# Reordering the beginning of a fused Fourier-filter and MoE kernel: x on one queue, zeros on TensorE, filters in x's place, weights' bits off GpSimd's queue

## The chip, the cores and the metric

The kernel runs on one core of one Trainium2 chip. A core has five engines that take their own instruction streams in order: TensorE (PE in the profile; PEld is its weight load), VectorE (DVE), ScalarE (ACT), GpSimd (POOL) and SyncE (SP). SP, ScalarE and GpSimd can each issue DMAs from their stream; "SPq" is SP's part as a queue of DMA issues. The metric is the device time of one execution in microseconds; the time before is 2791.76 us, the median of three runs (2789.57 to 2792.46).

## What is computed

The reference, cut to what matters (x and the filters are float32, the two weights arrive as 64-bit floats and the kernel computes in float32; eight batches of 3008 positions and 256 channels; hidden width 2048):

```python
X = np.fft.rfft(x, axis=1)                 # x: (8, 3008, 256)
F = (filt_r + 1j * filt_i)[None, :, :]     # (1505, 256)
y = np.fft.irfft(X * F, n=3008, axis=1)
t = y.reshape(24064, 256)
h = t @ w_in                               # (256, 2048)
g = h * np.clip(h + 3.0, 0.0, 6.0) / 6.0
out = g @ w_out                            # (2048, 256)
```

## The kernel before

**The Fourier part.** 3008 = 47 x 64, so each transform is done in two factors as matrix products with constant tables. For a batch, `a_unit` multiplies the 47 rows of x (for two halves of 32 columns j) with table `wa`; the result goes to DRAM as `z_tmp` (`z_store`) and comes back with another axis on the partitions (`t2_load`). `b_unit` (L350) multiplies with table `wb`, `f_unit` (L362 to L364, VectorE) applies the filter tile `ft`, `bi_unit` (L382) goes back with table `wi`, `g_store` writes `g_tmp` in DRAM. `t4_load` (L413) reads it back, and `n_unit` (L420) makes the last product with `wai` and leaves transposed tokens in `xn`, which the MoE part reads in blocks of 512. `wb` and `ft` come in six parts c of four frequencies (`table_load`: four filter DMAs and one of `wb`); two buffers of each exist (`FB` = 2).

**The first batch** takes another way into this, since nothing can hide it. `x0_load` reads batch 0 into 94 partitions (rows 0 to 46 for the half h = 0, 47 to 93 for h = 1), 28 of its 32 columns in the upper part of `w_all` (the place of the MoE weights, not yet filled) and 4 in a `t1` tile. h = 0 goes through SP's queue and h = 1 through ScalarE's. `a0_unit` (L295) multiplies each column with the 96-wide table in `start`, four columns to a PSUM bank, four banks in turn; ScalarE copies them (L297) into `xn` and `xs`, used as scratch. `turn` (L307) transposes them with an identity to where `b_unit` wants them, in place of the trip through DRAM. Then six rounds c follow, each with `turn(c+1)`, two `b_unit` and `f_unit`, and `bi_unit` and `g_store` of the round before, the stores from ScalarE's queue.

**The weights.** The 16 parts of `w_in` and `w_out` (eight pairs p) are loaded as pairs of 32-bit integer words ("bits", 512 KB each) and decoded to float32 by seven or eight VectorE operations (`w_conv`, L222 to L240), called a conversion here. Two are converted before the rounds, two within them, two after them and ten in the first steps of the MoE part. Their loads go through GpSimd's queue by default. `w_sums` (L247, GpSimd) then makes eight sums for a pair, which overwrite slot 1 of `w_in` and of `w_out`; so they are made two steps after the pair's plain use.

**The MoE part** is a loop over 47 blocks k and eight pairs p. Block 0 is plain: `plain_up` (L532), the activation (L490 on ScalarE, `hswish` L495 on VectorE), `plain_down` (L543). All later blocks use a seven-product scheme (L445 up, L521 down) which needs the sums. Other work is hung on numbered steps (k*8 + p) by `at(step, fn, ...)`; work of the same step runs in the order in which it was entered, `a_unit`, `b_unit`, `bi_unit` and `n_unit` early in the step and all other late. Batch 1's `a_unit` and `z_store` stand in steps 1 to 8, its first `b_unit` in step 11. The block's result goes out by `store`, 14 DMAs for block 0 on SP.

The order within each engine is the order of the program text (`manual_schedule`), and a queue's DMA that waits holds all that is behind it.

Of the kernel before, what the change touches and what calls it, by code (L numbers as in the profile page):

```python
# [32 lines left out]
HC = NC // 2  # L33
XC = 4
# [20 lines left out]
def _make_tables():  # L55
# [5 lines left out]
    for h in range(2):  # L61
        for k in range(KH):
            th = 2 * np.pi * ((a * k) % NA) / NA
            for g in range(2):
                wa[h * 64:h * 64 + NA, g * 64 + k] = np.cos(th)
                wa[h * 64:h * 64 + NA, g * 64 + 32 + k] = -np.sin(th)
            start[h * NA:(h + 1) * NA, P + 4 * k + h] = np.cos(th)
            start[h * NA:(h + 1) * NA, P + 4 * k + 2 + h] = -np.sin(th)
# [39 lines left out]
def kernel(  # L108
# [60 lines left out]
    def table_load(b, c):  # L169
        t = ft[(b * NT + c) % FB]  # L170
# [4 lines left out]
        wb = tabp.tile([P, TC, P], FP32, name="wb")  # L175
# [68 lines left out]
    def w_sums(p):  # L244
        for w, sums in ((w_in[p], IN_SUMS), (w_out[p], OUT_SUMS)):
            for o, x0, x1, op_ in sums:
                nc.gpsimd.tensor_tensor(out=w[:, o, :], in0=w[:, x0, :], in1=w[:, x1, :], op=op_)  # L247
# [11 lines left out]
    IN_SUMS = ((4, 1, 3, ALU.add), (1, 0, 1, ALU.subtract), (5, 4, 0, ALU.subtract), (6, 2, 5, ALU.subtract))  # L259
    B11, T3, B21, B22, T1, T2, T4 = range(7)  # L260
    OUT_SUMS = tuple((o, x0, x1, ALU.subtract) for o, x0, x1 in ((4, 1, 0), (1, 1, 3), (5, 3, 4), (6, 2, 5)))
# [13 lines left out]
    def x0_tile(j):  # L275
        if j < 28:
            return w_all.rearrange("p a b c m -> p (a b c m)")[:, 4 * 14 * P:].rearrange("p (j d) -> p j d", d=D), j
        return st["x0"], j - 28

    def x0_load(j, n):  # L280
        t, o = x0_tile(j)
        rows = x[0].rearrange("(a c) d -> a c d", c=NC)
        for r, m in ((0, 32), (32, NA - 32)):
            for h, q in ((0, nc.sync), (1, nc.scalar)):
                q.dma_start(t[h * NA + r:h * NA + r + m, o:o + n, :], rows[r:r + m, ds(h * HC + j, n), :])
# [4 lines left out]
    def a0_unit(j):  # L290
        for dh in range(2):
            ps = bank(0)
            for u in range(4):
                t, o = x0_tile(j + u)
                nc.tensor.matmul(ps[:, ds(u * 96, 96)], t[0:2 * NA, o, ts(dh, P)], st["start"][0:2 * NA, ds(P, 96)],  # L295
                                 start=True, stop=True)
            nc.scalar.activation(out=zt(dh).rearrange("p (n j) -> p j n", j=HC)[:, j:j + 4, :],  # L297
                                 in_=ps[:, 0:384].rearrange("p (j n) -> p j n", j=4), func=AXT.Copy)
# [34 lines left out]
    def z_store(b, c):  # L333
        t = st.pop(("t1", b, c))
        for g in range(2):
            for ri in range(2):
                p0 = g * 64 + ri * 32
                z = z_d[b, :, ts(ri, NC), :].rearrange("k (h j) d -> k h j d", h=2)
                nc.gpsimd.dma_start(z[:, :, ds(c * XC + 2 * g, 2), :], t[p0:p0 + KH, :, :, :])  # L339
# [14 lines left out]
    def f_unit(b, i):  # L354
        c, r = divmod(2 * i, TC)
        ps = st.pop(("ps", b, i))
        f = ft[(b * NT + c) % FB][:, r:r + 2, :]
# [50 lines left out]
    def t4_load(i, k0=0, k1=KH):  # L408
        b, j, n = chunks[i]
        for h in range(2):  # L410
            for ri in range(2):
                p0 = h * 64 + ri * 32
                nc.sync.dma_start(t4[i % 2][p0 + k0:p0 + k1, 0:n, :].rearrange("k j d -> k (j d)"),  # L413
# [197 lines left out]
    with tc.manual_schedule():  # L611

        st["start"] = p14p.tile([P, 2, 2, P], FP32, name="p14").rearrange("p a u m -> p (a u m)")
        st["x0"] = t1p.tile([P, 2, XC // 2, D], FP32, name="t1").rearrange("p a j d -> p (a j) d")
        nc.sync.dma_start(st["start"][:, 0:2 * P], start_d)
        nc.vector.memset(top_c, -0x40000000)
        nc.vector.memset(half_c, 0.5)
        for j in range(0, 24, 8):  # L620
            x0_load(j, 8)
        for j in 24, 28:
            x0_load(j, 4)
# [3 lines left out]
        def convert(n, act=True, most=NCONV, q=nc.gpsimd):  # L627
            nonlocal loaded, done
            for i in range(n + 1):
# [3 lines left out]
                if i < n:  # L633
                    w_conv(done, act)
                    done += 1

        convert(0, most=2)
        for t in t4:
            nc.gpsimd.memset(t, 0.0)
        for c in range(FB):  # L640
            table_load(0, c)
            convert(0, most=3 + c, q=nc.sync)
        for j in range(0, HC, 4):
            a0_unit(j)
        convert(2, False, 4)
        turn(0)
        for c in range(NT + 1):
            if c + 1 < NT:
                turn(c + 1)
            if c < NT:  # L650
# [3 lines left out]
                if c + FB < NT:  # L654
                    table_load(0, c + FB)
                if c in (1, 3):
# [178 lines left out]
```

## Time and profile before

| what | us |
|---|---|
| median of three runs | 2791.76 |
| the profiled execution | 2791.65 |
| its span, first to last instruction | 2789.9 |
| TensorE busy | 2714.4 (97%) |
| VectorE busy | 1940.1 (70%) |
| ScalarE busy | 1330.6 (48%) |
| GpSimd busy | 398.4 (14%) |

The marks of the beginning, by start in the timeline:

| mark | us |
|---|---|
| first L295 pass | 8.0 |
| first ScalarE copy L297 | 22.9 |
| first L307 pass | 44.4 |
| first L350 pass | 51.5 |
| last issue of a g_tmp store by ScalarE | 90.9 |
| first psn pass (L420) | 104.4 |
| first plain pass (L532) | 110.2 |
| first pass of the seven-product scheme (L445) | 187.3 |
| first L350 pass of batch 1 | 218.6 |

A float32 matmul shows as two passes in the trace, so counts there are twice those of the program. A row such as "PE po L295 <- ACT xn L297: 8.7, 1, 8.7" reads: TensorE stood for 8.7 us in total before instructions of line 295, once, until a ScalarE instruction of line 297 released it. The rows that carry the argument are shown with the prediction.

### The profile page before, as it was taken

How to read it: one execution, taken by the hardware profiler on the slowest of the kernel's cores; microseconds unless marked ns; L12 is line 12 of the kernel's file. 1: busy time of each engine (PE TensorE's matmuls, PEld its weight loads, DVE VectorE, ACT ScalarE, POOL GpSimd, SP SyncE). 2: the span in 40 equal slices, each digit the busy share in tenths (PEclk: the TensorE clock that was granted, in tenths of full speed). 3: DMA queues.
4: the chain of work that ended last, by engine and by line, in shares of the span. 5: the costliest groups of instructions: out<-in, count | busy, mean ns of one | idle time of the engine just before them, and what ended most of it. 6: DMA issues, size and time to landing. Idle time of an engine off the chain costs nothing.

```text
span 2789.9 us, 47067 instructions
## 1 busy us (share of the span) xinstructions
PE 2714.4 (97%) x18112; PEld 2420.2 (87%) x18112; DVE 1940.1 (70%) x3399; ACT 1330.6 (48%) x2663; POOL 398.4 (14%) x627
## 2 busy tenths in 40 slices
PE   7698999999999999999999999999999999999997
PEld 6367888989889998899988998899988999999997
DVE  3656765777657776677756777567775677766665
ACT  3233445454554445544455445544455444444443
POOL 0170112010120011201021101210012100000000
PEclk9899999999999999999999999999999999999999
DMA  6633223321323222322133221332123321110000
GB/s 156 190 85 108 66 62 85 85 77 44 80 60 90 74 53 71 88 62 79 46 88 87 72 57 46 86 91 71 49 55 91 98 60 47 36 31 23 19 9 16
DMA packets 117321, 194.73 MB, mean 70 GB/s; under 512 B 21843, under 2 KB 83251, under 8 KB 116687
## 3 DMA queue, kind: packets, MB, share of 16 engines
q1 hardware_dynamic: 93561, 136.24, 17.2%
q0 software_dynamic: 19456, 50.52, 7.8%
q10 hardware_dynamic: 4080, 4.96, 0.7%
q8 instruction: 143, 2.34, 0.4%
q14 instruction: 81, 0.66, 0.1%
HBM read 119.80 MB, written 71.83 MB: 69 GB/s over the span
## 4 chain that ended last, share of the span: by engine, by line
PE 93%; DVE 3%; DMA 2%; SPq 1%; POOL 1%; issue 0%; ACT 0%; POOLq 0%; ACTq 0%; DVEq 0%
PE po L521 41%; PE al L445 22%; PE be L445 17%; PE psn L420 4%; PE psf L350 3%; PE psf L327 2%; PE psf L382 2%; PE po L295 1%; DMA w_all<-in_x_dram 0%; SPq L413 0%; DVE g L495 0%; PE po L350 0%; DMA out_dram<-o 0%; DMA wb<-wb_t 0%; DVE y L224 0%
## 5 line engine op out<-in xcount | busy, mean ns | idle before, releaser
L521 PEld LDWEIGHTS po<-w_all,g 128*128 128x128 f32 x10304 | 1368.7, 191 | 143.4 <-issue 36.5
L521 PE MATMUL po<-w_all,g 128*128 128x128 f32 x10304 | 1399.1, 276 | 3.7 <-DVE g L495 3.3
L495 DVE SCALAR_TENSOR_TENSOR g<-r,h 128x512 f32<-128x512 f32 x736 | 506.7, 688 | 268.2 <-ACT r L490 255.2
L490 ACT ACTIVATE r<-h,half_c 128x512 f32<-128x512 f32 x736 | 531.1, 722 | 326.2 <-DVE h L471 314.1
L445 PE MATMUL al<-xt,w_all 128*128 128x256 f32 x2208 | 660.2, 381 | 1.5 <-DVE h L476 1.0
L471 DVE TENSOR_TENSOR h<-be,s 128x512 f32<-128x512 f32 x368 | 254.2, 691 | 271.4 <-PE be L445 260.0
L445 PE MATMUL be<-xn,w_all 128*128 128x256 f32 x1472 | 437.8, 379 | 0.0
L445 PEld LDWEIGHTS al<-xt,w_all 128*128 128x128 f32 x2208 | 335.5, 192 | 3.5 <-issue 1.3
L445 PEld LDWEIGHTS be<-xn,w_all 128*128 128x128 f32 x1472 | 279.7, 190 | 37.9
L485 ACT ACTIVATE h<-al 128x256 f32<-128x256 f32 x368 | 141.3, 384 | 350.5 <-PE al L445 350.5
L476 DVE TENSOR_TENSOR h<-al,s 128x256 f32<-128x256 f32 x368 | 156.3, 425 | 166.0 <-PE al L445 164.8
L503 DVE TENSOR_TENSOR g<-g 128x512 f32<-128x512 f32 x368 | 254.8, 692 | 12.6
L466 ACT ACTIVATE s<-al 128x256 f32<-128x256 f32 x368 | 141.4, 384 | 208.5 <-PE al L445 208.5
L457 ACT ACTIVATE s<-be 128x256 f32<-128x256 f32 x368 | 141.3, 384 | 176.4 <-PE be L445 176.4
L445 PE MATMUL al<-xn,w_all 128*128 128x256 f32 x736 | 219.9, 381 | 0.5 <-ACT h L485 0.5
L445 PE MATMUL be<-xt,w_all 128*128 128x256 f32 x736 | 218.9, 379 | 0.0
L339 POOL DMA_DIRECT2D z_tmp<-t x224 | 129.6, 583 | 412.1 <-ACT t L330 409.2
L456 ACT ACTIVATE s<-al 128x256 f32<-128x256 f32 x368 | 141.3, 384 | 71.0 <-PE al L445 71.0
L505 DVE TENSOR_TENSOR g<-g 128x256 f32<-128x256 f32 x368 | 160.8, 437 | 12.5
L502 DVE TENSOR_TENSOR g<-g 128x256 f32<-128x256 f32 x368 | 156.5, 425 | 12.6
L445 PEld LDWEIGHTS be<-xt,w_all 128*128 128x128 f32 x736 | 139.8, 190 | 18.9
L420 PEld LDWEIGHTS psn<-wai,t 128*128 128x128 f32 x1024 | 134.1, 195 | 22.2 <-issue 16.0
(106 smaller groups left out, 1793.5 us busy)
## 6 DMA issues: line engine op xcount, KB each, us to landing
t<-g_tmp SPq DMA_DIRECT2D x188, 120.0 KB
z_tmp<-t POOLq DMA_DIRECT2D x224, 96.0 KB, 2.9
t<-z_tmp SPq DMA_DIRECT2D x42, 512.0 KB
g_tmp<-t POOLq DMA_DIRECT2D x84, 256.0 KB, 3.8
out_dram<-o SPq DMA_DIRECT2D x321, 47.0 KB
xs<-in_x_dram SPq DMA_DIRECT2D x112, 128.0 KB
ft<-in_filt_r_dram SPq DMA_DIRECT2D x96, 128.0 KB
ft<-in_filt_i_dram SPq DMA_DIRECT2D x96, 128.0 KB
```

The costliest lines, as they stand in the source:

```text
L420: nc.tensor.matmul(ps[:, ts(q, TOK)], t4[i % 2][:, q, ts(dh, P)], wai[:, chunks[i][1] + q, :], start=True, stop=True)
L445: nc.tensor.matmul(ps, w_in[p][:, w, :], x, start=start, stop=stop, skip_group_check=True)
L456: nc.scalar.activation(out=s[:, 0, :], in_=al, func=AXT.Copy)
L466: nc.scalar.activation(out=s[:, 1, :], in_=al, func=AXT.Copy)
L471: nc.vector.tensor_tensor(out=st["h"][0].rearrange("p (a n) -> p a n", a=2), in0=be, in1=s, op=ALU.add)
L476: nc.vector.tensor_tensor(out=st["h"][1][:, 256:512], in0=al, in1=s5, op=ALU.add)
L490: nc.scalar.activation(out=r, in_=st["h"][i], func=AXT.Relu, bias=half_c, scale=1.0 / 6.0)
L495: nc.vector.scalar_tensor_tensor(out=st["g", k, p][:, o:o + 2, :].rearrange("p a n -> p (a n)"), in0=st["r", i], scalar=1.0, in1=st["h"][i ...
L502: v.tensor_tensor(out=g[:, G1, :], in0=g[:, G3, :], in1=g[:, G22, :], op=ALU.add)
L503: v.tensor_tensor(out=g[:, G3:G2 + 1:2, :], in0=g[:, G3:G1 + 1, :], in1=g[:, G11:G11 + 1, :].broadcast_to([P, 2, 256]), op=ALU.subtract)
L505: v.tensor_tensor(out=g[:, G4, :], in0=g[:, G12, :], in1=g[:, G2, :], op=ALU.subtract)
L521: nc.tensor.matmul(st["po", k][bank][:, part, u, :], g[:, a, ts(u, P)], w_out[p][:, w, :], start=(p == 0 and n in OPENS and u == 0), stop= ...
```

## The change

It has six parts. The first batch's x is loaded by SP alone, into partitions 0 to 46 and 63 to 109, in pieces of 4, 4, 8, 8 and 8 columns; partitions 47 to 62 get 16 rows of x once more, against which the table has zeros, so that a0 runs over 110 rows, and its products are 128 columns wide instead of 96. Five matmuls over a tile of zeros (one column of it is not zero) stand on TensorE ahead of a0, and ScalarE has a small copy ahead of its first real one. The filters and `wb` of rounds 2 to 5 are loaded into the place of x in `w_all`, all ahead of the rounds. Weights' bits are loaded through SP, but for the first two; three conversions stand before the rounds and two after, none within, and eleven in the MoE part; three sums follow each conversion and the fourth comes two steps after the use, as before. The first loads of `g_tmp` take 16 of 24 rows and stand a round earlier, and the rest goes through SP and ScalarE. Batch 1's `z_store` goes through SP, and its first two table loads stand in step 5 instead of step 9.

```diff
@@ -31,6 +31,7 @@
 DFF = 2048
 HALF = 64
 HC = NC // 2
+H1 = 63
 XC = 4
 NB = HC // XC
 TC = 4
@@ -64,8 +65,8 @@
             for g in range(2):
                 wa[h * 64:h * 64 + NA, g * 64 + k] = np.cos(th)
                 wa[h * 64:h * 64 + NA, g * 64 + 32 + k] = -np.sin(th)
-            start[h * NA:(h + 1) * NA, P + 4 * k + h] = np.cos(th)
-            start[h * NA:(h + 1) * NA, P + 4 * k + 2 + h] = -np.sin(th)
+            start[h * H1:h * H1 + NA, P + 4 * k + h] = np.cos(th)
+            start[h * H1:h * H1 + NA, P + 4 * k + 2 + h] = -np.sin(th)
     wb = np.zeros((P, KH, P))
     wi = np.zeros((P, 3, NC))
     re, im = slice(0, NC), slice(NC, P)
@@ -167,12 +168,17 @@
     def table_load(b, c):
-        t = ft[(b * NT + c) % FB]
+        if b == 0 and c >= FB:
+            at = x0_at(1536 * (c - FB), 1536)
+            t, wb = at[:, 0:1024].rearrange("p (k d) -> p k d", k=TC), at[:, 1024:].rearrange("p (k m) -> p k m", k=TC)
+        else:
+            t, wb = ft[(b * NT + c) % FB], tabp.tile([P, TC, P], FP32, name="wb")
+        st["ft", b, c] = t
         for src, p0 in ((filt_r, 0), (filt_i, HALF)):
             nc.sync.dma_start(t[p0:p0 + 32, :, :].rearrange("p k d -> p (k d)"),
                               raw(src, c * TC, [[NA * D, 32], [1, TC * D]]))
             nc.sync.dma_start(t[p0 + 32:p0 + 64, :, :], raw(src, NA - c * TC, [[NA * D, 32], [-D, TC], [1, D]]))
-        wb = tabp.tile([P, TC, P], FP32, name="wb")
         nc.sync.dma_start(wb, wb_d[:, ts(c, TC), :])
         st["wb", b, c] = wb
@@ -241,10 +247,10 @@
                                op0=ALU.is_ge, op1=ALU.mult)
-    def w_sums(p):
-        for w, sums in ((w_in[p], IN_SUMS), (w_out[p], OUT_SUMS)):
-            for o, x0, x1, op_ in sums:
-                nc.gpsimd.tensor_tensor(out=w[:, o, :], in0=w[:, x0, :], in1=w[:, x1, :], op=op_)
+    def w_sums(i, late):
+        w = (w_in, w_out)[i % 2][i // 2]
+        for o, x0, x1, op_ in (IN_SUMS, OUT_SUMS)[i % 2][3 * late:3 + late]:
+            nc.gpsimd.tensor_tensor(out=w[:, o, :], in0=w[:, x0, :], in1=w[:, x1, :], op=op_)
@@ -256,9 +262,9 @@
     A11, S3, A12, A22, S1, S2, S4 = range(7)
-    IN_SUMS = ((4, 1, 3, ALU.add), (1, 0, 1, ALU.subtract), (5, 4, 0, ALU.subtract), (6, 2, 5, ALU.subtract))
+    IN_SUMS = ((4, 1, 3, ALU.add), (5, 4, 0, ALU.subtract), (6, 2, 5, ALU.subtract), (1, 0, 1, ALU.subtract))
     B11, T3, B21, B22, T1, T2, T4 = range(7)
-    OUT_SUMS = tuple((o, x0, x1, ALU.subtract) for o, x0, x1 in ((4, 1, 0), (1, 1, 3), (5, 3, 4), (6, 2, 5)))
+    OUT_SUMS = tuple((o, x0, x1, ALU.subtract) for o, x0, x1 in ((4, 1, 0), (5, 3, 4), (6, 2, 5), (1, 1, 3)))
     G11, G3, G1, G2, G4, G12, G22 = range(7)
@@ -272,17 +278,17 @@
-    def x0_tile(j):
-        if j < 28:
-            return w_all.rearrange("p a b c m -> p (a b c m)")[:, 4 * 14 * P:].rearrange("p (j d) -> p j d", d=D), j
-        return st["x0"], j - 28
+    def x0_at(o, n):
+        return w_all.rearrange("p a b c m -> p (a b c m)")[:, ds(NP * 14 * P - HC * D + o, n)]
+    x0 = x0_at(0, HC * D).rearrange("p (j d) -> p j d", d=D)
     def x0_load(j, n):
-        t, o = x0_tile(j)
         rows = x[0].rearrange("(a c) d -> a c d", c=NC)
-        for r, m in ((0, 32), (32, NA - 32)):
-            for h, q in ((0, nc.sync), (1, nc.scalar)):
-                q.dma_start(t[h * NA + r:h * NA + r + m, o:o + n, :], rows[r:r + m, ds(h * HC + j, n), :])
+        for p, a, m, h in ((0, 0, 32, 0), (H1, 0, 32, 1), (32, 32, NA - 32, 0), (H1 + 32, 32, NA - 32, 1),
+                           (NA, 0, H1 - NA, 0)):
+            nc.sync.dma_start(x0[p:p + m, j:j + n, :], rows[a:a + m, ds(h * HC + j, n), :])
     def zt(dh):
         return (xn.rearrange("p a n -> p (a n)"), xs.rearrange("p i j d -> p (i j d)"))[dh]
@@ -291,11 +297,10 @@
         for dh in range(2):
             ps = bank(0)
             for u in range(4):
-                t, o = x0_tile(j + u)
-                nc.tensor.matmul(ps[:, ds(u * 96, 96)], t[0:2 * NA, o, ts(dh, P)], st["start"][0:2 * NA, ds(P, 96)],
+                nc.tensor.matmul(ps[:, ts(u, P)], x0[0:H1 + NA, j + u, ts(dh, P)], st["start"][0:H1 + NA, ts(1, P)],
                                  start=True, stop=True)
             nc.scalar.activation(out=zt(dh).rearrange("p (n j) -> p j n", j=HC)[:, j:j + 4, :],
-                                 in_=ps[:, 0:384].rearrange("p (j n) -> p j n", j=4), func=AXT.Copy)
+                                 in_=ps.rearrange("p (j n) -> p j n", j=4)[:, :, 0:4 * KH], func=AXT.Copy)
     def turn(c):
         t = t2p.tile([P, TC, D], FP32, name="t2")
@@ -330,13 +335,13 @@
             nc.scalar.activation(out=t[:, h, :, :].rearrange("p j d -> p (j d)"), in_=ps[h], func=AXT.Copy)
         st["t1", b, c] = t
-    def z_store(b, c):
+    def z_store(b, c, q=None):
         t = st.pop(("t1", b, c))
         for g in range(2):
             for ri in range(2):
                 p0 = g * 64 + ri * 32
                 z = z_d[b, :, ts(ri, NC), :].rearrange("k (h j) d -> k h j d", h=2)
-                nc.gpsimd.dma_start(z[:, :, ds(c * XC + 2 * g, 2), :], t[p0:p0 + KH, :, :, :])
+                (q or nc.gpsimd).dma_start(z[:, :, ds(c * XC + 2 * g, 2), :], t[p0:p0 + KH, :, :, :])
     def t2_load(b, c):
         t = t2p.tile([P, TC, D], FP32, name="t2")
@@ -354,7 +359,7 @@
     def f_unit(b, i):
         c, r = divmod(2 * i, TC)
         ps = st.pop(("ps", b, i))
-        f = ft[(b * NT + c) % FB][:, r:r + 2, :]
+        f = st["ft", b, c][:, r:r + 2, :]
         pool_, n1, n2 = (hp, "h0", "h1") if b == 0 and i & 2 else (sp, "s1", "s2")
         s1, s2 = (pool_.tile([P, 512], FP32, name=n).rearrange("p (u d) -> p u d", u=2) for n in (n1, n2))
@@ -405,12 +410,12 @@
         b, j, n = chunks[i]
         return b * N + j * TOK, n * TOK
-    def t4_load(i, k0=0, k1=KH):
+    def t4_load(i, k0=0, k1=KH, qs=None):
         b, j, n = chunks[i]
         for h in range(2):
             for ri in range(2):
                 p0 = h * 64 + ri * 32
-                nc.sync.dma_start(t4[i % 2][p0 + k0:p0 + k1, 0:n, :].rearrange("k j d -> k (j d)"),
+                (qs or (nc.sync, nc.sync))[ri].dma_start(t4[i % 2][p0 + k0:p0 + k1, 0:n, :].rearrange("k j d -> k (j d)"),
                                   g_d[b, k0 // 2:k1 // 2, ri, :, ds(h * HC + j, n), :].rearrange("i u j d -> i u (j d)"))
@@ -612,19 +617,23 @@
         st["start"] = p14p.tile([P, 2, 2, P], FP32, name="p14").rearrange("p a u m -> p (a u m)")
-        st["x0"] = t1p.tile([P, 2, XC // 2, D], FP32, name="t1").rearrange("p a j d -> p (a j) d")
         nc.sync.dma_start(st["start"][:, 0:2 * P], start_d)
+        for j, n in (0, 4), (4, 4), (8, 8), (16, 8), (24, 8):
+            x0_load(j, n)
+        zero = rp.tile([P, 512], FP32, name="r", tag="r")
+        nc.vector.memset(zero, 0.0)
         nc.vector.memset(top_c, -0x40000000)
         nc.vector.memset(half_c, 0.5)
-        for j in range(0, 24, 8):
-            x0_load(j, 8)
-        for j in 24, 28:
-            x0_load(j, 4)
+        nc.scalar.activation(out=zero[:, 0:1], in_=half_c, func=AXT.Copy)
+        warm = psF.tile([P, 512], FP32, name="psf", tag="f")
+        for i in range(5):
+            nc.tensor.matmul(warm, zero[:, P:2 * P], zero, start=True, stop=True)
         nc.scalar.dma_start(wi, wi_d)
         loaded = done = 0
-        def convert(n, act=True, most=NCONV, q=nc.gpsimd):
+        def convert(n, act=True, most=NCONV, q=nc.sync):
             nonlocal loaded, done
             for i in range(n + 1):
                 while loaded < most and w_before(loaded) < done:
@@ -632,17 +641,22 @@
                     loaded += 1
                 if i < n:
                     w_conv(done, act)
+                    w_sums(done, False)
                     done += 1
-        convert(0, most=2)
+        convert(0, most=2, q=nc.gpsimd)
         for t in t4:
             nc.gpsimd.memset(t, 0.0)
+        convert(0, most=3)
         for c in range(FB):
             table_load(0, c)
-            convert(0, most=3 + c, q=nc.sync)
         for j in range(0, HC, 4):
             a0_unit(j)
-        convert(2, False, 4)
+        for c in range(FB, NT):
+            table_load(0, c)
+            convert(0, most=min(c + 2, 6))
+        convert(3, False, 6)
+        nc.sync.dma_start(wai[:, 0:8, :], wai_d[:, 0:8, :])
         turn(0)
         for c in range(NT + 1):
             if c + 1 < NT:
@@ -651,34 +665,29 @@
                 for i in (2 * c, 2 * c + 1):
                     b_unit(0, i)
                     f_unit(0, i)
-                if c + FB < NT:
-                    table_load(0, c + FB)
-                if c in (1, 3):
-                    convert(1, False, 5 + c // 2, nc.sync)
-            if c == 3:
-                nc.sync.dma_start(wai[:, 0:8, :], wai_d[:, 0:8, :])
             if c:
                 bi_unit(0, 2 * c - 2)
                 g_store(0, 2 * c - 2, nc.scalar)
-            if c == NT - 1:
+            if c == NT - 2:
                 for i in range(2):
-                    t4_load(i, 0, KH - TC)
+                    t4_load(i, 0, KH - 2 * TC)
+        for i in range(2):
+            t4_load(i, KH - 2 * TC, KH, (nc.sync, nc.scalar))
         convert(2, False)
-        for i in range(2):
-            t4_load(i, KH - TC)
         for i in range(2):
             for dh in range(2):
                 n_unit(i, dh)
         nc.sync.dma_start(wai[:, 8:HC, :], wai_d[:, 8:HC, :])
+        nc.sync.dma_start(wa, wa_d)
         for c in range(3):
             x_load(1, c)
-        nc.sync.dma_start(wa, wa_d)
         for i in range(NCONV - done):
             at(i // 2, convert, 1)
         for p in range(NP):
-            at(p + 2, w_sums, p)
+            for i in range(2):
+                at(p + 2, w_sums, 2 * p + i, True)
         n_at = {0: -2, 1: -2}
         used = {}
@@ -715,7 +724,7 @@
             a_at, b_at, bi_at = places(n)
             for c, s in enumerate(a_at):
                 at(s, a_unit, n, c)
-                at(s, z_store, n, c)
+                at(s, z_store, n, c, nc.sync if n == 1 else None)
                 if c >= 3:
                     at(max(a_at[c - 3], s - 6), x_load, n, c)
                 elif n > 1:
@@ -723,7 +732,7 @@
             for c in range(NT):
                 s = b_at[2 * (c - TB) + 1] + 1 if c >= TB else a_at[-1] + 1
                 at(s, t2_load, n, c)
-                s = b_at[2 * (c - FB) + 1] + 1 if c >= FB else a_at[-1] + 1
+                s = b_at[2 * (c - FB) + 1] + 1 if c >= FB else a_at[-1 if n > 1 else 3] + 1
                 at(s, table_load, n, c)
             for i in range(NU):
                 at(b_at[i], b_unit, n, i)
```

## The prediction

> **What bounds the kernel now.** I read the page's slices first, then the waits of TensorE up to 104 us and from there to 420 us, then the chain of waits of the first 110 us. The page (busy tenths in 40 slices, one slice 70 us):
>
> ```profile
> PE   7698999999999999999999999999999999999997
> DMA  6633223321323222322133221332123321110000
> ```
>
> From slice 4 on TensorE is full and sets the time; a change to the beginning moves the end by what it takes off the first three slices. TensorE's waits (total us, times, longest), two answers:
>
> ```profile
> PE po L295 <- ACT xn L297: 8.7, 1, 8.7
> PE po L295 <- DMA w_all<-in_x_dram: 8.0, 1, 8.0
> PE po L350 <- DMA wb<-wb_t: 5.5, 3, 2.2
> ```
>
> ```profile
> PE psn L420 <- DMA t<-g_tmp: 14.2, 1, 14.2
> PE psf L350 <- DMA ft<-in_filt_r_dram: 7.2, 1, 7.2
> PE al L532 <- DVE g L495: 7.0, 3, 3.9
> ```
>
> The chain of waits (start us, us, what) tells why:
>
> ```profile
> 4.66 13.53 DMA w_all<-in_x_dram
> 18.21 3.39 DMA t<-in_x_dram
> 21.60 1.28 ACT L297
> ...
> 23.78 20.81 PE po L295 x96
> ...
> 47.14 1.71 PE be L307 x8
> ...
> 54.30 0.89 PE be L307 x8
> ...
> 103.37 1.01 DMA t<-g_tmp
> ```
>
> ScalarE issues half of x and is held by its queue, so its first copy comes at 22.9 us though TensorE had filled four banks by 15.1. Then 96 passes take 20.81 us (217 ns each), and those of L307 214 ns up to 50.8 us and 111 ns after: TensorE is at half speed until then. (The granted clock reads 1.00 in these first rows, so I go by passes; later, where it reads 0.50, passes have the same long times.) At the far end sixteen loads of one stage are issued one by one:
>
> ```profile
> 92.41 11.54 SPq L413 DMA_DIRECT2D t<-g_tmp  x16
> ```
>
> So the beginning has three stretches: x and a0 (to 45.4 us), turn/b/bi (last g_store issued at 90.9), stores and loads (psn at 104.4). After it the plain block is paced by VectorE's weight conversions, until 168.2 us.
>
> **Step 1: x, zeros, a0.** In the two-microsecond rows the DMA engines are full (share 0.93 to 1.10) from 2 to 24 us and move about 201 to 223 GB/s while x loads. New x is 110 rows of 32 KB, 3.60 MB, with 0.13 MB of start and 1.05 MB of GpSimd's bits beside it: 4.78 MB. At 210 GB/s from 2 us: 24.8 us; at the 257 to 338 GB/s of the 128-row loads at 24 to 32 us: 16 to 21. I take 23, nearer the x rows, since the pieces stay 32 and 15 rows. Here the skill speaks against the change: "SBUF — State Buffer", Door 1 (the DMA port swizzle), says bandwidth follows from how many of 16 ports the partitions reach, and partitions 0 to 63 share eight. Old rows: 64 of 94 on these; new: 64 of 110, the 16 fillers among them. By the rule alone nothing is gained and 0.52 MB more moves (2.5 us at 210); the hope is only that pieces of both halves now alternate in one queue. The 23 counts all bytes and half the hope.
>
> Zeros: memset, ScalarE's table load (1.28 us, now before x) and one copy give a start at about 2.7 us; ten passes of 512 columns at half speed take 8.5 us (the cold first 128x512 passes of L532 took 0.85 each), till 11.2, less if the clock comes on. Will it stay on for a0? The skill, "TensorE: Matmul & The Clock Gate", Part 1, says some 3.4 us of activity bring full clock. The trace differs: L295 (94 rows, 96 columns) ran 20.8 us without a break and stayed slow; L307 (128 by 128) needed 6.4 us, L532 at 168 us about 3.3. By the rule a0 would warm by itself and the zeros bring nothing; by the rows it never does in its old shape. I follow the rows: zeros warm it, and the 128-wide passes, in which a load of 128 columns sets the 214 ns anyway, cost no more than 96-wide and keep it. Gaps between x pieces are about 1 us (8 columns of x: 0.90 MB, 4.2 us, against 3.4 us of passes); it stayed warm over 1.9 us at 60.8 and lost it in 2.2 us before 81.6.
>
> So a0 follows x: after the last piece 32 passes x 0.107 = 3.4 us and one copy, 0.83: 27.4 us, where before it was 45.4. **Gain 18.**
>
> **Step 2: turn, b, bi.** Per round warm: turn 16 x 0.111 = 1.78, b 1.74, bi 1.87: 5.39 us; six rounds 32.3, about 2 for first and last copies, 1.1 for the last pair: last g_store issued 35.5 after a0's end; before 45.5 (90.9 - 45.4). VectorE no longer stops for two conversions (4.4 us each) between rounds; its 4.25 us a round fit. The filters of rounds 2 to 5 no longer wait for a freed buffer but for a0's reading of that part of x, long done. The third conversion stands ahead of the first f_unit on VectorE: its bits follow x on SP, land about 27, done 31.5; f_unit wants to start near 32, so it costs nothing unless x is late, then about as much as x. But bytes get tight: up to the last g_store 15.2 MB (14.8 by the rows to 90 us, 0.5 more); after 23 us 10.4 MB at 240 GB/s (rows from 60 to 80: 235, 246) end at 66 us, TensorE's own chain at 68 with landing. Two limits 2 us apart wait for one another; I charge 4 (bounds 0 and 8; the old wb waits were 5.5). **Gain 6.**
>
> **Step 3: stores to psn.** Now only eight loads follow the last store, four on each of two queues: issue 1.3, landing 3.4 (the store on the chain at 88.9), four issues at 0.65, landing 1.0: 8.3 us against 13.5. The first eight loads hide behind the last two rounds; if SP were late with them the gain is 0. ScalarE waits in these loads, but behind it stand only the copies of psn, which need them too. **Gain 5.2**; psn at about 75.
>
> **Step 4: plain block (before: 104.4 to 187.3).** Eleven conversions remain instead of ten; the extra one falls in step 5, between two hswish, where a TensorE step of 8.1 us (172 to 180) covers 4.2. Three of four sums now follow each conversion on GpSimd. Clear steps took 9.9 us; with GpSimd busy 10.8 and 12.3, VectorE's 690 ns operations growing to 820 and 1,090. Now each of five such steps has some 5 us of sums. Bounds: -3 (no worse than the clear steps) and +9 (all as the worst); near the 10.8 row I charge **+3**. The 0.5 us that L445 waited for sums goes.
>
> Loads and z_stores pass from GpSimd to SP. SP is in order: bits 6 and 7 follow the eight late loads; bits 8 wait for conversion 4, and wai (1.1 MB), wa and twelve x loads stand behind. That conversion ends near 72 us, before the late loads are out: no wait. wa and the first x are due at psn + 13.9 and come 0 to 2 us late, inside TensorE's idle time of that step (2.3 us). Bits 9 hold SP for conversion 5, with the loads of the next psn behind: due two steps, 20 us, later. Each z_store waits for ScalarE's copy and holds bits that are four or five conversions early.
>
> **Step 5: second batch's tables.** Issued in step 5, ten DMAs leave the place behind the 14 out stores (194.4 to 208.1) where TensorE stood 7.2 us. But the last z_store now sits there: 2.4 us of issue, 2.5 of landing, then the z load, 0.5 MB. From the block's end: outs to 20.8, z_store landed 26, z load landed 29.5; TensorE asks at 24.1 and got it at 31.3. **Gain 1.5** (bounds +8 gain, 5 loss).
>
> **Sum:** 18 + 6 + 5.2 - 3 + 1.5 = 27.7 us off 2791.65 of the profiled execution (span 2789.9; 1.75 lie around it; the runs' median is 2791.76): **2764 us**.
>
> **Rivals.** (a) **The clock does not come, or is lost between pieces of x.** Zeros end at 11.2, 128 passes x 0.213 + copy: 39.4 us, 12 later; first turns slow, 3 more; but the byte limit's 4 go, and step 3 stays: about 17 off, 2775. For it: the 20.8 us of slow passes, and the 2.2 us gap; against: 512-column passes warmed in every later place. (b) **One queue carries x too slowly.** Before, two queues shared the rate; at 130 GB/s for start and x: 31 us, 8 later: 2772. Against it: the engines were full, and an SP-only row at 210 us shows 328 GB/s. (c) **GpSimd's sums** slow every conversion as the worst step: 9 instead of 3, and in the first rounds as much again: 2776. (d) **The other side: conversions starve behind SP.** Ten bits loads (6 to 15) come behind z_stores and x loads; each that reaches its turn less than 5.2 us (landing of such a load) ahead stops VectorE, the bound of this block. All ten in full: +52, so 2816; slower from 2.8 us each. For it: SP had 12 x loads spread over 23.7 us waiting for buffers there; against: the distance of four conversions, about 20 us.
>
> **Numbers.** Forecast 0.57, (a) 0.20, (b) 0.10, (c) 0.06, (d) 0.05, gains used up to no change 0.02. Low end: x by 18 us and no byte wait, 9 better: 2755. High end: past (a) and (c): 2780. About 0.2% (5.6 us) is what can be told from no change: faster 0.92, within 0.02, slower 0.06.
>
> **What would show it.** L312's first passes at 111 ns and a0's last copy near 27 us (step 1; near 39 is (a)); last g_store issued near 67 (2); psn near 75 with eight late loads (3); first L450 about 86 us after psn (4), above 92 is (c) or (d), told apart by whether VectorE is slow or waits for bits; L355's wait about 5 us (5). The forecast falls if TensorE is slow at 20 to 40 us or VectorE waits for DMA in the plain block.

## The result

The changed kernel takes 2764.77 us, the median of four runs (2764.24 to 2765.29), against 2791.98 us before (2789.57 to 2792.46, four runs): a ratio of 0.9904 with a 95% interval of 0.9887 to 0.9921, 27.2 us less. The forecast was 2764. Its profiled execution has a span of 2763.1 us, 26.8 less than before.

The page of the changed kernel, in the slices shown before (busy tenths in 40 equal parts of the span):

```profile
PE   8789999999999999999999999999999999999998
DMA  8632223221332213322133212332123321110000
```

Only the first slices have moved. TensorE's waits in the changed kernel, up to 80 us in the first block and from 80 to 420 us in the second (total us, times, longest):

```profile
PE po L300 <- DMA w_all<-in_x_dram: 3.2, 2, 2.3
PE po L355 <- DMA w_all<-wb_t: 2.4, 2, 1.7
```

```profile
PE psn L425 <- DMA t<-g_tmp: 12.3, 1, 12.3
PE al L537 <- DVE g L500: 6.9, 3, 3.8
PE psf L355 <- DMA t<-z_tmp: 5.5, 1, 5.5
```

The 8.7 us for ScalarE are gone, those for `wb` have more than halved (5.5 to 2.4), and the wait of batch 1's first `b_unit` is now for `z_tmp` instead of the filters. The wait for `g_tmp` is nearly as long as before, but it ends at 80 us instead of 104.

The span can be cut at marks that both traces have (start of the first or last instruction of its kind, us; a0's end is the end of its last copy):

| stretch | before | after | gain | forecast |
|---|---|---|---|---|
| start to a0's last copy | 45.4 | 30.4 | 15.0 | 18 |
| to the last issue of a g_tmp store | 45.5 | 40.3 | 5.2 | 6 |
| to the first psn pass | 13.5 | 9.4 | 4.1 | 5.2 |
| to the first pass of the seven-product scheme | 82.9 | 84.5 | -1.6 | -3 |
| to batch 1's first b_unit | 31.3 | 29.6 | 1.7 | 1.5 |
| to ScalarE's output copy of the last block | 2554.7 | 2555.5 | -0.9 | 0 |
| to the end | 16.6 | 13.4 | 3.2 | 0 |
| sum | 2789.9 | 2763.1 | 26.8 | 27.7 |

The middle 2,550 us repeat to within a microsecond, as a stretch bound by TensorE should. But the beginning gave 24.4 of a forecast 27.7, and 3.2 came at the end, where nothing had been forecast.

One mark hides something. In the changed kernel ScalarE's last copies in the rounds end at 68.4 us, but it issues the store of their result only at 70.65:

```profile
67.33 1.09 ACT L390 ACTIVATE t<-psf 128x512 f32<-128x512 f32 x2 [1.57 <-PE psf L387]
70.65 1.27 ACTq L397 DMA_DIRECT2D g_tmp<-t  x2
```

Before, the issue followed the copies at once (90.90 and 90.93). So 2.2 us of new waiting are counted in the second stretch, and from the end of the copies to psn it is 11.6 us against 13.5, a gain of 1.9 and not of 4.1.

In the changed kernel a0 does not quite go as the forecast had it. Its TensorE work, merged in the timeline (start us, us, line, operation, tiles, shape, count, what ended the idle time before it):

```profile
2.29 7.36 PE L632 MATMUL psf<-r 128*128 128x512 f32 x10 [2.29 <-ACT r L629]
10.52 4.05 PE L300 MATMUL po<-p,w_all 110*128 110x128 f32 x32 [0.88 <-DMA w_all<-in_x_dram]
16.92 12.58 PE L300 MATMUL po<-p,w_all 110*128 110x128 f32 x96 [2.35 <-DMA w_all<-in_x_dram]
```

and by stretches of two microseconds (PE busy and passes, granted clock, DMA share, GB/s):

```profile
14.00:16.00 2.00, 0.58 (x6) 1.00 0.98 193
16.00:18.00 2.00, 1.08 (x9) 1.00 1.01 217
18.00:20.00 2.00, 2.00 (x13) 0.55 0.98 193
20.00:22.00 2.00, 2.00 (x13) 0.60 0.98 220
22.00:24.00 2.00, 2.00 (x21) 1.00 0.97 182
```

The zeros did bring full clock: 32 passes of a0 take 4.05 us with their gaps. Then TensorE is through with what has come and stands 2.35 us for the third piece of x. It goes on at full clock for a little over 1 us, drops to half at 18.2 and is back at full at 21.6 (0.55 and 0.60 in the two slices, 13 passes in 2 us where a full clock has 21). What was gained up to 14.6 us is lost by 22.

### The profile page after: what moved, and what is told of

Same layout as the page of the kernel before. It is cut to its first block, busy times and chain, and to the rows that moved or that the text cites. A ratio compares the mean times of both kernels' runs of the same rounds, so it can differ in the third digit from the quotient of the medians.

```text
span 2763.1 us, 47097 instructions
## 1 busy us (share of the span) xinstructions
PE 2708.6 (98%) x18122; PEld 2409.1 (87%) x18122; DVE 1941.5 (70%) x3399; ACT 1332.5 (48%) x2665; POOL 373.6 (14%) x585
## 3 DMA queue, kind: packets, MB, share of 16 engines
q0 software_dynamic: 16480, 42.13, 6.7%
## 4 chain that ended last, share of the span: by engine, by line
PE 93%; DVE 3%; DMA 2%; SPq 0%; issue 0%; ACT 0%; POOL 0%; POOLq 0%; DVEq 0%; ACTq 0%
PE po L526 41%; PE al L450 23%; PE be L450 17%; PE psn L425 4%; PE psf L355 3%; PE psf L332 2%; PE psf L387 2%; DMA w_all<-in_x_dram 0%; PE po L300 0%; DMA w_all<-wb_t 0%; DVE g L500 0%; DVE y L230 0%; PE po L548 0%; PE al L537 0%; DVE y L243 0%
## 5 line engine op out<-in xcount | busy, mean ns | idle before, releaser
L450 PE MATMUL al<-xt,w_all 128*128 128x256 f32 x2208 | 660.5, 381 | 1.5 <-DVE h L481 1.0
L450 PE MATMUL be<-xn,w_all 128*128 128x256 f32 x1472 | 438.3, 379 | 0.0
L450 PEld LDWEIGHTS al<-xt,w_all 128*128 128x128 f32 x2208 | 335.5, 192 | 3.5 <-issue 2.2
L450 PEld LDWEIGHTS be<-xn,w_all 128*128 128x128 f32 x1472 | 280.0, 190 | 38.0
L450 PE MATMUL al<-xn,w_all 128*128 128x256 f32 x736 | 219.9, 381 | 0.5 <-ACT h L490 0.5
L450 PE MATMUL be<-xt,w_all 128*128 128x256 f32 x736 | 218.9, 379 | 0.0
L344 POOL DMA_DIRECT2D z_tmp<-t x192 | 111.1, 587 | 411.3 <-ACT t L335 409.1
L450 PEld LDWEIGHTS be<-xt,w_all 128*128 128x128 f32 x736 | 139.8, 190 | 18.9
```

Of the source, the lines that this page charges most:

```text
L450: nc.tensor.matmul(ps, w_in[p][:, w, :], x, start=start, stop=stop, skip_group_check=True)
```

## The experiments

Each is an edit of the changed kernel but for one, which edits the kernel before. Times are medians of few runs; the marks of one profiled execution say where a difference arose. The kernel before, timed anew beside each group of them, had medians from 2790.6 to 2792.0 us, so a difference of 1 to 2 us between times of different groups says nothing by itself. The first four ask what brings the clock, and whether the queue matters.

**Zeros and width, two by two.** Without the zeros:

```diff
-        for i in range(5):
-            nc.tensor.matmul(warm, zero[:, P:2 * P], zero, start=True, stop=True)
+        nc.tensor.matmul(warm[:, 0:1], zero[:, P:2 * P], zero[:, 0:1], start=True, stop=True)
```

> Leaves out four and a half of the five matmuls on zeros (one column of one remains); the output is the same. Theory (clock by shape and gaps): a0's first passes are slow (213 ns), 128-wide passes bring full clock only after some 6 us of unbroken work, which the gaps between the pieces of x interrupt; a0's last copy near 34 us instead of 30.4, time 3 to 5 us above the changed kernel's 2764.8. Rival (some 3.4 us of any activity bring full clock): last copy within 1.5 us of 30.4, time within 1.5 us.

With the zeros, but 96 columns to a product:

```diff
-                nc.tensor.matmul(ps[:, ts(u, P)], x0[0:H1 + NA, j + u, ts(dh, P)], st["start"][0:H1 + NA, ts(1, P)],
+                nc.tensor.matmul(ps[:, ds(u * 96, 96)], x0[0:H1 + NA, j + u, ts(dh, P)], st["start"][0:H1 + NA, ds(P, 96)],
```

> Zeros kept, a0's products 96 columns wide again. Theory: the clock that the zeros bring is lost in the gap of 2.4 us before the third piece of x (14.6 to 16.9 us), and 96-wide passes do not bring it back: 96 passes at 213 ns after 16.9, last copy near 38 us, time 7 to 9 us above 2764.8. Rival (width is nothing): last copy at 30.4, same time.

And with both edits:

> No zeros and 96 columns. Theory: all 128 passes of a0 at 213 ns, last copy near 39 us, first turn slow too: time 9 to 12 us above 2764.8, a few us more than with zeros and 96 columns. Rival (3.4 us of any activity): no more than 3 us above.

| | 128 columns | 96 columns |
|---|---|---|
| zeros: a0's last copy | 30.4 | 36.6 |
| no zeros: a0's last copy | 29.4 | 39.1 |
| zeros: time | 2764.8 | 2773.9 |
| no zeros: time | 2764.5 | 2773.0 |

Width is worth 8.5 to 9 us of time and the zeros nothing. My theory had it right for 96 columns and wrong for the zeros, with which 96 columns were no faster than without. (96 and 128 are the columns of the table that a pass streams. The weights in the array, which are x here, are 110 by 128 in all four kernels, as the "110*128" of the rows says.) The timeline of the kernel without zeros:

```profile
10.40 5.34 PE L300 MATMUL po<-p,w_all 110*128 110x128 f32 x32 [7.53 <-DMA w_all<-in_x_dram]
16.68 7.67 PE L300 MATMUL po<-p,w_all 110*128 110x128 f32 x64 [0.93 <-ACT xs L302]
24.71 3.81 PE L300 MATMUL po<-p,w_all 110*128 110x128 f32 x32 [0.37 <-DMA w_all<-in_x_dram]
```

The first passes are slow, and just therefore they fill the time until the third piece of x is there: no gap over 1 us is left, and the 110 by 128 passes bring full clock by themselves at 13.6 us. With zeros and 96 columns the clock is lost after the same gap as in the changed kernel, and does not come back in a0; without zeros it never comes:

```profile
16.20 19.55 PE L300 MATMUL po<-p,w_all 110*128 110x96 f32 x96 [2.17 <-DMA w_all<-in_x_dram]
```

```profile
10.67 27.59 PE L300 MATMUL po<-p,w_all 110*128 110x96 f32 x128 [7.80 <-DMA w_all<-in_x_dram]
```

The first has its clock at half from 17.5 us on, the second takes 216 ns a pass for 27.6 us without a break. So activity alone does not bring the clock, whether it lasts the 3.4 us that the prediction quotes from the Trainium skill ("TensorE: Matmul & The Clock Gate", Part 1) or eight times that; the shape decides.

**x on two queues.**

```diff
-            nc.sync.dma_start(x0[p:p + m, j:j + n, :], rows[a:a + m, ds(h * HC + j, n), :])
+            (nc.sync, nc.scalar)[h].dma_start(x0[p:p + m, j:j + n, :], rows[a:a + m, ds(h * HC + j, n), :])
```

with x's loads in the program behind the zeros, so that ScalarE's table load and small copy stay ahead of them.

> The half h = 1 of x goes through ScalarE's queue again, after ScalarE's table load and small copy; all else as changed. Theory: ScalarE's copies wait until its last x issue, near 18 to 20 us, x itself lands no earlier; sixteen copies of 0.87 us then end near 34 us: time 3 to 5 us above 2764.8. Rival (one queue carries x slower than two): x lands earlier by more than the copies lose, last copy before 30 us, time at or under 2764.8.

The first copy comes at 17.6 us instead of 11.7 and the last at 33.2 instead of 30.4. The time is 2766.6, the median of two runs 3 us apart (2765.0 and 2768.2), 1.8 more where 3 to 5 were expected. x's first piece came sooner than by one queue (TensorE goes from the zeros straight to it at 9.24, instead of 10.52), its third later:

```profile
18.55 13.81 PE L300 MATMUL po<-p,w_all 110*128 110x128 f32 x96 [2.80 <-DMA w_all<-in_x_dram]
```

So two queues did not carry x faster to where TensorE waits for it, and the rival falls. But the theory is not borne out either: TensorE waits for none of the copies that ScalarE's queue held. The 2.8 us by which a0 ends later are the later third piece (18.55 instead of 16.92) and the clock, which goes at 14.3, ahead of that wait, and comes back at 24.5 instead of 21.6 (13.81 us for 96 passes instead of 12.58). What the held copies cost in the kernel before, whose row shows 8.7 us, no run isolates.

**Rows of x.**

```diff
-H1 = 63
+H1 = 47
...
-                           (NA, 0, H1 - NA, 0)):
```

> x on one queue but in the 94 rows of before (0 to 46 and 47 to 93, no filler rows, 0.52 MB less); products still 128 wide. Theory of the prediction (half the hope for ports): placement is worth something, so the 15% fewer bytes buy little: third piece of x near 16 us against 16.9, last copy within 1 us of 30.4, time within 1.5 us of 2764.8. Rival (bytes at about 210 GB/s are all that counts): x lands 2 us earlier, last copy near 28 us, time about 2 us under. Second rival (the new rows do spread the ports): x lands later in spite of fewer bytes, last copy after 32 us.

This run answered another question than it was asked. The pieces of x come earlier with fewer bytes: TensorE's first pass is at 8.96 us instead of 10.52, its pass on the third piece at 16.05 instead of 16.92. There is no sign that the rows' new places carry x faster. But the time is 2773.1 us, 8 us more, and a0's last copy at 37.7:

```profile
16.05 20.82 PE L299 MATMUL po<-p,w_all 94*128 94x128 f32 x96 [0.94 <-DMA w_all<-in_x_dram]
```

```profile
28.00:30.00 2.00, 2.00 (x11) 0.50 1.05 220
30.00:32.00 2.00, 2.00 (x12) 0.50 1.08 206
32.00:34.00 2.00, 2.00 (x11) 0.50 0.94 209
```

Over 94 rows even 128 columns do not bring the clock, in 20.8 us without a break. None of the three expectations saw this. The filler rows, which I had counted as 0.52 MB of cost, are what makes a0 fast, together with the width.

**The filters' place.**

```diff
-        if b == 0 and c >= FB:
+        if False:
...
                     f_unit(0, i)
+                if c + FB < NT:
+                    table_load(0, c + FB)
```

with the loads ahead of the rounds left out.

> Filters and wb of rounds 2 to 5 go into two buffers in turn and are loaded within the rounds, as before; the bits of conversions 3 to 5 stay ahead of them. Theory: each of the four loads can start only when the f_unit two rounds earlier is done and takes 3 to 4 us to land while VectorE and TensorE need 5.4 us a round, so TensorE waits about 2 us in each of four rounds; but the changed kernel waits 2.4 us there itself for its bytes: last g_store 4 to 7 us later than 70.65, time 4 to 7 us above 2764.8. Rival (DMA bytes are the limit of this stretch whatever the buffers): last g_store within 2 us of 70.65.

The theory falls: the last store is issued at 69.0 us, not 4 to 7 us after the changed kernel's 70.65, and the time is 2764.0 us. But part of this is a0. This execution kept full clock all through it, though TensorE waited 2.17 us for the third piece of x:

```profile
16.00 3.81 PE L300 MATMUL po<-p,w_all 110*128 110x128 f32 x32 [2.17 <-DMA w_all<-in_x_dram]
```

a0 ended at 29.1 instead of 30.4. From there to the last store it is 39.9 us against 40.3, with 4.1 us of waiting for `wb` against 2.4 and without the 2.2 us in which ScalarE held the store. x's place for the filters brings nothing that can be told. The rival's reason, that bytes are the limit of this stretch, fits but is not isolated by this run.

**The sums beside each conversion.**

```diff
-                    w_sums(done, False)
...
+                at(p + 2, w_sums, 2 * p + i, False)
                 at(p + 2, w_sums, 2 * p + i, True)
```

> All eight sums of a pair come two steps after its plain use again, as before; everything else as changed. Theory: the sums beside every conversion cost the plain block 2 to 3 us, so the stretch from the first psn to the first L450 shrinks from 84.5 to 81 to 83 us, if GpSimd, now free of DMAs, ends its sums in time; time 1 to 3 us under 2764.8. Rival (sums bunched later slow the last conversions more and TensorE waits for sums at L450): the stretch is 84.5 us or longer, time at or above 2764.8.

From the first psn to the first L450 pass it takes 80.8 us against 84.5: the theory holds, and TensorE waits nowhere for GpSimd. Of the 3.7 us, 1.5 are shorter waits for VectorE's `hswish` (6.9 to 5.4 us) and 2.2 are TensorE's own passes (busy 77.4 to 75.2 us, at a granted clock of 0.88 and 0.90). The time, 2763.5 us, is only 1.3 lower because in this execution the last store was issued at 72.6, 2 us later, in a part that the edit touches little (0.7 of it in a0, where the clock was lost for longer). So 3.7 us is what the early sums cost in their place; the times alone would not have shown it.

**The loads of g_tmp.**

```diff
-            if c == NT - 2:
+            if c == NT - 1:
                 for i in range(2):
-                    t4_load(i, 0, KH - 2 * TC)
+                    t4_load(i, 0, KH - TC)
...
-            t4_load(i, KH - 2 * TC, KH, (nc.sync, nc.scalar))
+            t4_load(i, KH - TC)
```

> The first loads of g_tmp take 20 of 24 rows and stand a round later, and the last four rows go through SP alone, as before. Theory: sixteen issues of 0.6 to 0.7 us, half of them after the last store, make psn start 3 to 5 us later against the last g_store (12 to 14 us instead of 9.4); time 3 to 5 us above 2764.8. Rival (the store's landing, not the issues, is what psn waits for): psn starts 9 to 10 us after the last g_store as now, time within 1 us.

The queue of SP in this kernel shows the old picture:

```profile
71.93 12.00 SPq L418 DMA_DIRECT2D t<-g_tmp  x16
```

psn starts 13.1 us after the last store's issue instead of 9.4, and the time is 2767.4 us, 2.6 more, a little under the 3 to 5 expected. The theory holds for the issues. But the store is issued 0.03 us after its copies here, not 2.2, so from the copies on the new loads are worth 1.5 us. In nine of the ten traces in which the early loads of `g_tmp` stand ahead of the last store it is held 2.2 to 3.9 us (in the tenth, the filters' run, 0.03), and in the three without them 0.03: they are the likely cause, by a link that the traces do not name.

**One part alone on the kernel before: the shape of a0.** The kernel before gets the 110 rows, the filler and the 128 columns, and keeps its two queues and everything else.

```diff
-                q.dma_start(t[h * NA + r:h * NA + r + m, o:o + n, :], rows[r:r + m, ds(h * HC + j, n), :])
+                q.dma_start(t[h * 63 + r:h * 63 + r + m, o:o + n, :], rows[r:r + m, ds(h * HC + j, n), :])
+        nc.sync.dma_start(t[NA:63, o:o + n, :], rows[0:63 - NA, ds(j, n), :])
```

> The kernel before with one part of the change alone: a0 over 110 rows and 128 columns, filler rows loaded, x still on two queues and ScalarE's copies still held till 22.9. Theory (share of the array that a pass uses decides the clock, 94 x 128 or 110 x 96 do not bring it, 110 x 128 does): passes drop to 107 ns some 3 to 4 us after 23.8, a0's last copy near 36 to 38 us instead of 45.4, time 7 to 10 us under the kernel before. Rival (the rows' placement or the single queue is needed for the clock): last copy at 45, same time.

2780.8 us against 2790.55 of the kernel before, timed beside it, a ratio of 0.9964 (0.9951 to 0.9978), and a0's last copy at 36.2. The shape alone is worth 9.7 us, over a third of the whole change. In its trace a0 gains 9.2 us and the rounds 3.2 (42.3 instead of 45.5 us to the last store), since their first products now run at full clock; about 1.5 are given back behind them. Full clock came at 17.6 us, just as the first 32 passes ended, went while TensorE waited 3.1 us for ScalarE's first copy, and came again only between 26 and 28 us:

```profile
24.00:26.00 2.00, 2.00 (x11) 0.50 1.00 189
26.00:28.00 2.00, 2.00 (x12) 0.54 1.04 161
28.00:30.00 2.00, 2.00 (x21) 1.00 1.07 159
```

**The last z_store.**

```diff
-                at(s, z_store, n, c, nc.sync if n == 1 else None)
+                at(s, z_store, n, c, nc.sync if n == 1 and c < NB - 1 else None)
```

> From the changed kernel, only the last z_store of batch 1 goes back to GpSimd's queue, ahead of the out stores in time. Theory: the first L355 pass of batch 1 follows the first L450 pass by 25 to 26.5 us instead of 29.6, since the z loads wait only for the out stores; time 3 to 4 us under 2764.8. Rival (the z loads are held by the out stores on the same engines, not by the z_store): 29 us or more, same time.

The stretch is 26.0 us instead of 29.6 and the time 2761.2 us. TensorE's wait for the z load in this kernel:

```profile
PE psf L355 <- DMA t<-z_tmp: 1.9, 1, 1.9
```

5.5 us have become 1.9: the z_store behind the 14 out stores was the new wait that took most of what the earlier tables gave.

**Together.** Zeros out, x in eight pieces of four columns, the sums late, the last z_store on GpSimd:

```diff
-        for j, n in (0, 4), (4, 4), (8, 8), (16, 8), (24, 8):
+        for j, n in [(j, 4) for j in range(0, HC, 4)]:
```

and the edits shown above.

> From the changed kernel: zeros left out as in the first experiment, x in eight pieces of four columns, all sums two steps after the plain use, and the last z_store of batch 1 on GpSimd. Theory (each measured or read alone: zeros 0 to 1 us, sums 3 to 4, the z_store behind the out stores 3 to 4, finer pieces 0 to 2): 7 us faster than 2764.8, 2757 to 2760. Rival (the parts overlap: an earlier step is lost to the same wait on DMA or VectorE): 2761 to 2764.

2756.4 us (2754.96 to 2759.69 in four runs), 0.9878 of the kernel before (0.9861 to 0.9896): 8.3 us under the changed kernel, whose runs all lie above these. (The two intervals against the kernel before overlap at their edges, and the two versions were not timed side by side.) The marks say where: a0 ends at 28.3 instead of 30.4, the plain block takes 80.2 instead of 84.5, the stretch to batch 1's `b_unit` 25.9 instead of 29.6. The rounds give back over half of what a0 gains: from a0's last copy to the last store it is 41.5 us instead of 40.3. (So they did with the zeros alone left out: a0 ended 1.0 us earlier and the last store was issued 0.1 earlier.)

## Why the prediction was right, and where it was not

**a0, gain 18 forecast, 15.0 measured.** "a0 follows x" is right: without the zeros TensorE waits for the last piece at 24.7 us, and the last copy ends 4.7 us later; the sum had 23 and 4.4 (its two terms make 4.2). What was mis-sized is x, by 1.7 us, because "half the hope" for the ports was granted: the rate is 182 to 220 GB/s from 14 to 24 us, as before (182 to 252). The rule on ports that I weighed, by which nothing was to be gained from the rows' places, was the better guide; all bytes at 210 GB/s made 24.8. The other microsecond is the step that failed: "**zeros warm it**, and the 128-wide passes ... keep it". They warm it, the gap ahead of the third piece (2.35 us, where I had put 1) takes it away for 3.4 us, and the zeros are worth nothing. The 1 us set 8 columns of x against the passes of 8; but the third piece follows one of 4, with 1.7 us of passes against 4.2 of loading, so the same figures make 2.5. Nor would a kept clock have paid: in the run with the filters in the rounds it held, and a0 ended at 29.1, without zeros at 29.4. The sum came out nearly right because the new shape restored what the gap took.

**The clock.** To follow the rows and not the rule of some 3.4 us was right, as the runs at 96 columns show, and it was the better part of this step. But I read the rows as "94 rows, 96 columns" without asking which of the two it was. It takes both: 110 by 96 and 94 by 128 stay slow. And a gap's length does not say whether the clock goes: 1.9 us kept it before and 2.2 lost it, but 1.77 and 1.91 us lost it (the runs with the last z_store on GpSimd and with two queues) and 2.17 us kept it (filters in the rounds).

The traces say more, though no run was made to test it. In all thirteen the granted clock changes only at whole steps of 3.41 us (at 18.20 and 21.61 in the changed kernel, at 15.92 and 22.75 with the sums late), from a start that differs from run to run. For each such period I took the share of it that passes fill, times their rows over 128, times their columns over 128 where they stream fewer than 128. This estimate from the first 230 us of the thirteen traces divides them well: clock was lost after periods of up to 0.42 and kept from 0.42 on; it was gained after periods of 0.81 and more, and half speed stayed up to 0.84. Unbroken passes of 110 by 128 make 0.86, of 94 by 128 0.73, of 110 by 96 0.64. The gap of 2.35 us falls into one period and leaves it 0.32 (1.77 us: 0.41); the one of 2.17 us is shared by two periods, 0.47 and 0.70.

**The rounds, 6 forecast, 5.2 measured.** About 2.5 us of it are the first `turn` at full clock, the gain of the shape (a0's last copy to the first `b_unit`: 3.6 us instead of 6.1), and 3.1 the shorter waits for `wb`; against them stand the 2.2 us in which ScalarE holds the last store, which the sum did not have. The charge of 4 us for tight bytes is borne out in part: TensorE waits 2.4 us for DMA there. That the filters' new place belongs to the gain was never claimed with a number, and moving them back changes nothing that can be told.

**Stores to psn, 5.2 forecast, 4.1 measured**, from the issues, as worked out: undone, it gives back 3.7 of these. Of the four terms, issue and landing of the store took 4.1 us (4.7 forecast), the four loads 3.5 (2.6) and the last landing 1.8 (1.0). Counted from the copies, 1.9 us were gained, since the store is held; the sum left that out.

**The plain block, -3 forecast, -1.6 measured.** The mechanism is GpSimd beside VectorE, 3.7 us when undone. With the sums back in their old place the stretch is 80.8 us, 2.1 shorter than before although it holds one conversion more, and 1.6 of that are shorter waits for VectorE (7.0 to 5.4): some other part of the change gained these 2 us, and no run says which. The 0.5 us that L445 waited for sums did not go; the same pass now waits as long for ScalarE. The bits on SP starved nothing: VectorE's waits from 60 to 170 us name no DMA at all, so rival (d) falls by the trace.

**The tables in step 5, 1.5 forecast, 1.7 measured**, with the z_store as the thing that is late next.

**What the sum lacked** is the end, 3.2 us. GpSimd's own rows at the last line of the program (count, shortest/median/longest ns), before and after:

```profile
L830 POOLq DRAIN  x3: 40/102/9303, 2779.8 to 2789.6; - x3
```

```profile
L839 POOLq DRAIN  x3: 40/102/6117, 2756.2 to 2762.8; - x3
```

The closing drain on GpSimd lasts 9.3 us before and in the one experiment on the kernel before, and 6.0 to 6.4 in the changed kernel and its ten variants. GpSimd's queue carried 19,456 packets in the former and 16,480 or 16,672 in the latter. That the drain goes with what this queue has carried fits and was not tested; the part of the change that does it, most likely the bits and z_stores taken off GpSimd, stays open.

So the total was hit with two misses of opposite sign, about 3 us each: the beginning 3.3 short, the end 3.2 over. That they cancel, and with it the agreement to 1 us, is luck.

## What to carry to other kernels

When TensorE runs at half speed though it is busy, look at the shape of its passes before adding work to warm it: filling rows against zeros in the table and streaming 128 columns instead of 96 cost no TensorE time here (213 to 217 ns a pass at half speed either way) and were worth 8 to 10 us. A held engine costs nothing if another limit ends close behind: with x on two queues the first copy was held until 17.6 us, and TensorE waited for x until 18.5. Take a mark where the work ends as well as where its result is sent off; the 2.2 us of the held store stood between the two. And of a step moved to another queue, count what it now stands behind, up to the last instruction of the program.

## What the runs showed of the hardware that was not expected

- TensorE's clock came or failed with the shape of the passes. At half speed throughout, without a break: 94 rows by 96 columns (20.8 us), 110 by 96 (27.6 us), 94 by 128 (20.8 us). Brought to full speed: 110 by 128 and 128 by 128. The columns are those streamed; the weights were 128 columns wide in all. Rows times columns lies at 0.73 of 128 by 128 or less in the first group and 0.86 or more in the second. The periods estimated above fit the product, with a limit between 0.81 and 0.84; no run was made to test it.
- It changed only at whole steps of 3.41 us. Coming to full speed with 110 by 128 passes took from 3.2 us (from 10.4, without zeros) to 6.6 (from 16.2, sums late). Gaps of 1.77 to 2.35 us ahead of a piece of x lost it in six kernels, one of 2.17 us did not in a seventh.
- The clock did not need data: 128 by 512 passes over zeros (but for one column) brought it (granted 1.00 and 0.43 us a pass from about 8 us on).
- A closing drain on GpSimd of 9.3 or some 6 us is part of the measured time.
